# Batch 0's second half of x: one GpSimd transfer of four heads, or two of two heads

## The chip, the cores and the metric

The kernel runs on one core of a Trainium2 chip. The metric is device time in microseconds of one execution. The kernel before took 219.81 us in the median of three runs (219.65 to 220.38).

## What is computed

The reference has two stages. The first is attention in both directions between tokens x (8 batches, 8 heads, 512 tokens, 64 wide) and a small state (32 rows for each batch and head). The second is a feed-forward layer with a ReLU gate over all 8 x 544 rows of 512.

```
scores  = scale * x @ state^T      a  = softmax(scores)     xread = a  @ state
scores2 = scale * state @ x^T      a2 = softmax(scores2)    sread = a2 @ x
h   = concat(xread, sread) as 4352 rows of 512
out = (relu(h @ w_gate) * (h @ w_val)) @ w_out              # w_gate, w_val: 512 x 1536
```

## The kernel before, in words

The order of all work is written out by hand: a string of steps (L455 on) for the first part, then a loop with units at fixed places. Each engine executes its instructions in that order. The kernel never forms xread: it multiplies the state with the gate and value weights (`u_mm`, L291, into `U`) and applies the attention weights `ANS` to that (`gv_mm`, L323), gates the result (`relu` L351 on ScalarE, `mult` L356 on VectorE) and multiplies by `w_out` (L363).

The change lies in the prologue, which brings the first data in:

- Batch 0's x comes in two ways. Heads 0 to 3 are loaded as float32 in two transfers, from SyncE's and ScalarE's queues (L420), and cast to bfloat16 by ScalarE and VectorE (`x_conv_pair`, L144). Heads 4 to 7 are loaded by one transfer of GpSimd's queue, which casts on the way (L427).
- GpSimd then makes the identity matrix `id128` (L428, rows of masks.py) that all transposes on TensorE use, and issues the rest of the loads in this order: batch 1's x in two transfers of four heads (`x_load`, L430 to 434: steps `dx.1.0.2 dx.1.1.2`), the gate and value weights in column pieces of 128 and 256 (`w_dma`, L108 to 110: steps `dw`), batch 2's x (`dx.2.0.1`), the rest of the state (`ds`), and `w_out` (`do`).
- The transfers of GpSimd's queue take eight semaphores in turn. A transfer waits, at its issue, until the eighth one before it has landed.
- TensorE first runs warm-up matmuls (`spin`, L438), which compute nothing that is used; they stand between steps as well. It transposes the state (L123), then x in groups (`x_T`, L156 to 162): `xT.0.0.4` and `xT.0.4.4` for heads 0 to 3, score matmuls for these (`att_sc`, L172 to 179, `sc.0.0`), `xT.0.8.4` for heads 4 and 5, `xT.0.12.4` for heads 6 and 7, then `xT.1.0.8` for the first half of batch 1, `sc.0.1`, `sc.1.0`, `xT.1.8.8`, and the first products with weights (`c_unit`, L312: `c.0.0.128`, then `c.1.128.128`).
- VectorE and ScalarE copy each group out of PSUM (`x_out`, L165), take exponentials (L206), sums and reciprocals (L212, L214).

The four steps of the program's string that follow `sc.0.0` on TensorE are in these lines:

```
spin.1.384
xT.0.8.4@4 xT.0.12.4@5 xo.0.8.4.act xo.0.12.4.act spin.1 xT.1.0.8@6 sc.0.1@1 ex.0.1 xo.1.0.8.dve spin.1
```

Of the kernel before, what the change touches and what calls it, by code (L numbers as in the profile page):

```python
# [16 lines left out]
def kernel(  # L17
# [9 lines left out]
    nc = tc.nc  # L27

    B, H, S, D = x.shape
# [4 lines left out]
    NC = S // 128  # L34
# [21 lines left out]
    HK = H // NK  # L56
# [21 lines left out]
    xf, xb, xT, eT, e_sn, a_sn, ANS, U, hsb = {}, {}, {}, {}, {}, {}, {}, {}, {}  # L78
# [26 lines left out]
    def xb_alloc(b):  # L105
        xb[b] = att.tile([128, H, NC, D], BF16, name="xb", tag="xb", bufs=4)
# [317 lines left out]
        w_dma((moe_w_gate, moe_w_val)[w], (wg_sb, wv_sb)[w], lo, lo + n)  # L424

    xb_alloc(0)
    nc.gpsimd.dma_start(out=xb[0][:, HK:H], in_=x[0, HK:H].rearrange("h (p c) d -> p h c d", c=NC))  # L427
    make_identity(nc, id128)  # L428

    def x_load(b, part, parts):  # L430
# [172 lines left out]
```

## Time and profile before

| what | value |
|---|---|
| median of the runs | 219.81 us (219.65 to 220.38) |
| profiled execution, its own time | 219.39 us |
| its span, first to last instruction | 217.6 us |
| TensorE busy | 212.8 us, 98% of the span |
| VectorE, ScalarE, GpSimd busy | 135.0, 117.8, 42.5 us |
| granted TensorE clock | 1.000 |
| GpSimd's DMA queue | 9.05 MB, 31.0% of the 16 engines' span |

The profile shows one execution. A page lists busy time by engine, the span in 40 slices, the DMA queues, the chain of work that ended last, and groups of instructions; other views of the trace list instructions in order of time with what each waited for, or busy time in chosen stretches. PE is TensorE's matmuls, PEld its weight loads, DVE is VectorE, ACT ScalarE, POOL GpSimd, SP SyncE. "L162" is line 162 of the kernel. A row such as `2.67 1.50 POOL L434 ... x2` is a group that starts at 2.67 us and spans 1.50 us; brackets hold the idle time before it and what ended it. A DMA's issue is a short row on its engine; its landing is later, and is recorded by the semaphore that it raises.

### The profile page before, as it was taken

The page shows a single profiled execution, that of the slowest core. Times are in us where ns is not written, and L with a number is a line of the kernel's source. Part 1 is how long each engine was busy: PE and PEld are TensorE (multiplying, and loading weights), DVE is VectorE, ACT ScalarE, POOL GpSimd, SP SyncE. Part 2 cuts the span into 40 slices and gives each one's busy share as a digit, 9 for nine tenths or more (in the row PEclk, how much of TensorE's full clock was granted, in tenths as well). Part 3 has the DMA queues.
Part 4 walks back from the last instruction along what each step waited for, and adds up shares of the span by engine and source line. Part 5 has one row for each costly group of instructions (what it writes and reads, how often), then busy time and mean ns, then how long its engine had stood idle before and what let it go on. Part 6 is the DMA issues. An engine that isn't in the chain of part 4 may idle for free.

```text
span 217.6 us, 4865 instructions
## 1 busy us (share of the span) xinstructions
PE 212.8 (98%) x1952; PEld 104.8 (48%) x1952; DVE 135.0 (62%) x233; ACT 117.8 (54%) x225; POOL 42.5 (20%) x63
## 2 busy tenths in 40 slices
PE   8899999999999999999999999999999999999994
PEld 4554454454444444444444444444544445666543
DVE  4799967956887678557966796388745444222100
ACT  4798877747546556455555656454646443333221
POOL 7974049005600531020107000000000000000000
PEclk9999999999999999999999999999999999999999
DMA  7999999579963995919491453131311122222132
GB/s 168 180 196 197 202 221 171 78 139 188 152 175 74 144 186 110 167 52 193 99 148 60 110 134 96 49 99 50 84 28 51 48 48 50 61 56 80 51 96 96
DMA packets 47399, 24.96 MB, mean 115 GB/s; under 512 B 27824, under 2 KB 43056, under 8 KB 47376
## 3 DMA queue, kind: packets, MB, share of 16 engines
q0 software_dynamic: 16896, 9.05, 31.0%
q1 hardware_dynamic: 29584, 14.85, 28.7%
q10 hardware_dynamic: 896, 0.75, 1.3%
q8 instruction: 15, 0.25, 0.4%
q14 instruction: 8, 0.07, 0.2%
HBM read 18.35 MB, written 8.91 MB: 125 GB/s over the span
## 4 chain that ended last, share of the span: by engine, by line
PE 96%; DVE 1%; ACT 1%; issue 0%
PE o_ps L367 40%; PE gv_ps L325 38%; PE gv_ps L347 5%; PE up L298 4%; PE warm_ps L440 2%; PE upc L298 2%; PE o_ps L396 1%; PE sr_ps L265 1%; PE sc_ps L179 1%; PE sT_ps L189 1%; PE xT_ps L162 1%; ACT e_sn L206 1%; DVE xT L165 1%; ACT xT L165 0%; PE aT_ps L234 0%; DVE cs L212 0%
## 5 line engine op out<-in xcount | busy, mean ns | idle before, releaser
L367 PE MATMUL o_ps<-wo_sb,h_sb 128*128 128x512 bf16 x372 | 94.3, 379 | 0.0
L325 PE MATMUL gv_ps<-ans,U 128*128 128x512 bf16 x384 | 93.2, 379 | 0.0
L358 DVE TENSOR_TENSOR h_sb<-gv_ps,g_sb 128x512 bf16<-128x512 f32 x96 | 65.1, 688 | 42.8 <-ACT g_sb L354 41.3
L354 ACT ACTIVATE g_sb<-gv_ps 128x512 bf16<-128x512 f32 (+1 forms) x108 | 61.7, 578 | 51.4 <-PE gv_ps L325 39.1
L325 PEld LDWEIGHTS <-U 128*128 128x128 bf16 x384 | 37.1, 98 | 44.5 <-issue 0.8
L367 PEld LDWEIGHTS <-h_sb 128*128 128x128 bf16 x372 | 35.2, 98 | 42.0 <-issue 4.0
L310 DVE CAST U<-up 128x512 bf16<-128x512 f32 x44 | 27.7, 684 | 5.7 <-PE up L298 5.7
L375 ACT COPY o_sb<-o_ps 128x512 f32<-128x512 f32 x31 | 18.4, 594 | 19.7 <-PE o_ps L367 17.7
L310 ACT CAST U<-up 128x512 bf16<-128x512 f32 x28 | 14.7, 595 | 8.8 <-PE up L298 8.8
L254 POOL COPY xa<-xb 128x1024 bf16<-128x1024 bf16 x16 | 16.0, 1045 | 10.0 <-PE sr_ps L265 5.9
L358 DVE TENSOR_TENSOR hs_sb<-gv_ps,g_sb 128x256 bf16<-128x256 f32 x12 | 5.1, 425 | 15.3 <-PE gv_ps L347 10.4
L212 DVE TENSOR_REDUCE cs<-e_sn 128x16 f32<-128x512 bf16 x16 | 10.8, 677 | 1.1 <-ACT e_sn L206 1.1
L218 DVE TENSOR_TENSOR a_sn<-e_sn,rc 128x512 bf16<-128x512 bf16 x16 | 10.9, 687 | 0.4
L298 PEld LDWEIGHTS <-stT 64*32 64x32 bf16 x560 | 6.7, 91 | 6.4 <-issue 5.3
L320 ACT CAST U<-upc 128x512 bf16<-128x512 f32 (+1 forms) x19 | 8.7, 522 | 1.7 <-PE upc L298 1.7
L446 POOL COPY mark<-g_sb 128x1 bf16<-128x1 bf16 x4 | 0.8, 190 | 41.8 <-ACT g_sb L354 41.8
L197 ACT ACTIVATE eT<-sT_ps 128x512 bf16<-128x512 f32 x10 | 5.4, 594 | 5.3 <-PE sT_ps L189 5.3
L434 POOL DMA_DIRECT2D xb<-in_x_dram x8 | 6.8, 847 | 3.1 <-DMA wg_sb<-in_moe_w_gate_dram 1.4
L347 PE MATMUL gv_ps<-br,wg_sb 128*128 128x256 bf16 x48 | 7.2, 273 | 0.0
L347 PE MATMUL gv_ps<-br,wv_sb 128*128 128x256 bf16 x48 | 7.2, 273 | 0.0
L399 DVE COPY o_sb<-o_ps 128x64 f32<-128x64 f32 x2 | 0.4, 224 | 10.6 <-PE o_ps L396 10.5
L298 PE MATMUL up<-wg_sb,stT 64*32 64x512 bf16 (+1 forms) x168 | 6.9, 348 | 0.0
(59 smaller groups left out, 124.1 us busy)
## 6 DMA issues: line engine op xcount, KB each, us to landing
out_dram<-o_sb SPq DMA_DIRECT2D x26, 256.0 KB, 2.4
xb<-in_x_dram POOLq DMA_DIRECT2D x6, 512.0 KB, 7.1
wo_sb<-in_moe_w_out_dram POOLq DMA_DIRECT2D x2, 768.0 KB, 10.5
out_dram<-o_sb SPq DMA_DIRECT2D x11, 128.0 KB, 2.4
wg_sb<-in_moe_w_gate_dram POOLq DMA_DIRECT2D x5, 256.0 KB, 9.4
wv_sb<-in_moe_w_val_dram POOLq DMA_DIRECT2D x5, 256.0 KB, 10.0
xb<-in_x_dram POOLq DMA_DIRECT2D x3, 256.0 KB, 5.3
st_f<-in_state_dram POOLq DMA_DIRECT2D x1, 384.0 KB, 11.4
```

Of the source, the lines that this page charges most:

```text
L212: nc.vector.reduce_sum(out=cs, in_=e_v, axis=AX.X)
L218: {"dve": nc.vector, "pool": nc.gpsimd}[eng].tensor_tensor(out=a_sn[b][:, jp].rearrange("p c (j n) -> p c j n", n=Ns), in0=e_v, in1=held[" ...
L254: nc.gpsimd.tensor_copy(out=v[:, hs], in_=xb[b][:, hs])
L298: nc.tensor.matmul(dst[kc][i0:i0 + 32], stT[r:r + 64, parity, b, h], wsb[r:r + 64, j, lo:lo + n], start=True, stop=True)
L310: copy[eng](out=U[b][:, w, kc, lo:lo + 512], in_=held["u", b, w, lo][kc])
L320: copy[eng](out=U[b][:, :, kc, lo:lo + n], in_=held["c", b, lo][kc])
L325: nc.tensor.matmul(ps[w], U[b][:, w, kc, f0:f0 + 128], ANS[b][:, kc].rearrange("p c t -> p (c t)"), start=(kc == 0), stop=(kc == NK - 1))
L347: nc.tensor.matmul(ps[w][:, 0:nt], wsb[:, j, f0:f0 + 128], br[:, j].rearrange("p b n -> p (b n)"), start=(j == 0), stop=(j == NJ - 1))
L354: nc.scalar.activation(out=g_sb[:, 0:n], in_=ps[0][:, 0:n], func=AF.Relu)
L358: nc.vector.tensor_tensor(out=dst, in0=ps[1][:, 0:n], in1=held["g", b, jf][:, 0:n], op=ALU.mult)
L367: nc.tensor.matmul(held["o", b, tsub], src[:, jf, tsub * 128:(tsub + 1) * 128], wo_sb[:, jf], start=(jf == 0), stop=(jf == NF - 1))
L375: copy[eng](out=o_sb, in_=held["o", b, tsub])
```

## The change

One transfer of heads 4 to 7 becomes two: heads 4 and 5, then heads 6 and 7. Both are issued by GpSimd one behind the other, at the same place. The bytes and the tile stay the same, and all lines behind move down by one.

```diff
     xb_alloc(0)
-    nc.gpsimd.dma_start(out=xb[0][:, HK:H], in_=x[0, HK:H].rearrange("h (p c) d -> p h c d", c=NC))
+    for j in range(2, 4):
+        nc.gpsimd.dma_start(out=xb[0][:, 2 * j:2 * j + 2], in_=x[0, 2 * j:2 * j + 2].rearrange("h (p c) d -> p h c d", c=NC))
     make_identity(nc, id128)
```

## The prediction

> **What bounds the kernel now.** I read the page first: its engine table and its chain of work that ended last. TensorE is busy 98% of the span, and the chain lies on it for 96%.
>
> ```profile
> PE 212.8 (98%) x1952; PEld 104.8 (48%) x1952; DVE 135.0 (62%) x233; ACT 117.8 (54%) x225; POOL 42.5 (20%) x63
> ...
> PE 96%; DVE 1%; ACT 1%; issue 0%
> ```
>
> The time can change where TensorE still waits: the prologue. So I read the timeline of the first 30 us next (start, duration, engine, line, then what it waited for), and in it what GpSimd issues, and where TensorE meets x.
>
> ```profile
> 1.25 0.89 POOL L427 DMA_DIRECT2D xb<-in_x_dram x1 [0.81 <-POOLq L587]
> ...
> 2.13 0.22 POOL masks.py:197 MEMSET id<- 128x128 bf16 x1
> 2.43 0.29 POOL masks.py:199 TENSOR_SCALAR_AFFINE_SELECT id<-id 128x128 bf16<-128x128 bf16 x1
> ...
> 2.67 1.50 POOL L434 DMA_DIRECT2D xb<-in_x_dram x2
> ...
> 6.83 0.59 PEld L162 LDWEIGHTS <-xb 128*128 128x128 bf16 x8
> ...
> 7.96 0.45 PEld L162 LDWEIGHTS <-xb 128*128 128x128 bf16 x8 [0.48 <-DMA xb<-in_x_dram]
> ...
> 8.38 0.25 DVE L214 RECIPROCAL rc<-cs 128x16 f32<-128x16 f32 x1
> ...
> 8.66 0.69 DVE L165 COPY xT<-xT_ps 128x1024 bf16<-128x1024 bf16 x1
> ...
> 10.75 0.25 PE L298 MATMUL upc<-wv_sb,stT 64*32 64x128 bf16 x8
> ```
>
> L427 is the transfer that the change splits; the two of L434 are batch 1's halves. The weight loads at 6.83 are for batch 0's heads 4 to 7, and stand there with no wait. The next eight, for batch 1's heads 0 to 3, do wait for their DMA.
>
> Third, the stretches of 1 us (engines' busy time, clock, DMA share, GB/s):
>
> ```profile
> 3.00:4.00 1.00, 1.00 (x2) 0.10 (x1) 0.50 (x2) 0.17 (x1) 1.00 (x2) 1.00 1.10 373
> 4.00:5.00 1.00, 1.00 (x7) 0.61 (x6) 0.28 (x1) 0.63 (x2) 1.00 (x3) 1.00 1.39 202
> 5.00:6.00 1.00, 1.00 (x11) 0.90 (x9) 0.54 (x2) 0.57 (x1) 1.00 (x2) 1.00 1.42 190
> ```
>
> From 3 us on the DMA engines have more than one packet each in hand without a break (share over 1). So what lands when is set by the order and the bytes in GpSimd's queue, not by the moment of issue, as long as the queue holds work.
>
> Fourth, the trace's records of each transfer's semaphore give its landing: batch 0's heads 4 to 7 at 6.57; batch 1's halves at 7.92 and 9.25; the first four weight pieces of 128 KB at 9.98, 10.71, 11.46, 12.19; pieces of 256 KB at 13.53 and 14.86. Transfers of 256 KB follow each other by 1.33 to 1.35 us: the engines' rate, about 195 GB/s.
>
> **What TensorE can bear.** Heads 4 to 7 landed 0.26 us before TensorE came to them (6.83 - 6.57). Batch 1's first half has less room than its wait suggests. Its eight transposes end at about 8.59, and their copy on DVE starts at 8.66, behind a reciprocal that ends at 8.63; so some 0.05 us may be lost there before the path moves. The second weight piece landed at 10.71 and its matmul stands at 10.75, with some 0.08 us to spare before the score matmuls at 11.41, which wait for ACT. The fourth landed at 12.19, its matmul is at 12.26: 0.08 again. Hence a rule for this prologue: **if GpSimd's stream as a whole slips by d, the end moves by d less about 0.07 us; if it comes earlier, at most about 0.1 us is won**, since DVE and ACT are next.
>
> **The change, part by part.**
>
> Removed: one transfer of four heads (512 packets of 512 B, issue 0.89 us). Added: two of two heads, 256 packets each, the same bytes; one issue; 16 completion packets; one TensorE wait, ahead of the transposes of heads 6 and 7. Nothing is reordered: the instruction lists of the two kernels differ in that issue and wait, and in which semaphore each later GpSimd transfer uses.
>
> The added issue. Rows: 0.75 and 0.76 us for the next two transfers of 512 packets, 0.89 for the first, 0.75 for st_f's 384 packets. No row has 256. Bounds 0 and 0.89; I take 0.75, the nearest row. All that GpSimd does behind it moves 0.75 us later:
> - The identity is ready at 3.47 in place of 2.72. Its first reader is the state transpose, for which TensorE is free only at 4.53, when the warm-up matmuls end. Hidden, 1.06 us to spare; without the warm-up the cover would be the state's own load, which leaves 0.4.
> - Batch 1's first half is issued at 3.42, not 2.67. Its packets must be ready when the packets ahead run out. The packet records of GpSimd's queue show the first at 3.89, 2.64 us after the issue; four later transfers into an idle queue (issued at 51.7, 70.6, 84.4 and 107.4) needed 1.58 to 1.62. Fifteen of the sixteen engines pass on from the four heads at 5.25 to 5.60, the last at 6.24. At 1.60 the packets are there at 5.02, 0.23 us early: hidden. At 2.64 they are there at 6.06, and the fifteen run dry for 0.46 to 0.81 us. I take 1.60, because the 2.64 belongs to the first transfer of the program, which is still the same one.
> - Batch 1's second half (4.18) and the weight pieces (from 4.91) stand behind over 1 us of queued bytes each: hidden. GpSimd itself catches up where it waits for the eighth transfer before to land: 0.56 us before its issue at 13.81, 0.59 before 15.14.
> - The eight-deep reuse of semaphores keeps its distance: each later transfer waits for the same transfer as before. The two that newly wait for the halves, near 7.8 and 8.5, come after 6.57 either way, or wait hundredths.
>
> The added completion. Batch 0's transfer and batch 1's follow at 1.35, others at 1.33: 0.02 us for a boundary. The other end: two pieces of 128 KB take 0.72 to 0.75 each, together 0.13 more than one of 256 KB, though they also have twice the packets per byte, which the halves of x do not. Bounds 0 to 0.13, taken 0.02. Here a rule speaks against the change. The Trainium skill, "DMA: Bandwidth & Descriptors", section "Anatomy of one DMA — SWDGE (gpsimd) path", gives each such transfer a fixed 2.0 us beside its bytes, and "Rules for kernel authors" says to coalesce small transfers into a large one. Paid one after the other it would put 2 us on the sum by an estimate from that page; the trace disagrees, since transfers here land 0.72 us apart.
>
> The first packet may come a little earlier, as a smaller list is written: 0.89 less 0.75 is 0.14 us at most by the rows of issue. That is no gain, by the rule above.
>
> The added wait. The eight loads at 6.83 took 0.59 us with one wait among them, those at 7.96 and 9.63 0.45 and 0.46: bounds 0 to 0.13 us, taken 0, since the second half lands before the loads are reached. Behind it stand heads 6 and 7, a warm-up matmul, batch 1's transposes; the wait at 7.96 swallows up to 0.1.
>
> What the split gives: heads 4 and 5 land some 0.7 us sooner (128 KB at 195 GB/s), near 5.9. Nobody reads them before 6.83. Gain 0.
>
> Sum: d = 0.02, less 0.07 of room: 0. The profiled execution took 219.39 us (span 217.6), the median of the runs is 219.81. Sum on the first 219.4; on the median, which is what will be compared, **219.8**. All the bounds together, without a dry queue: -0.1 and +0.2 (0.13 + 0.13 - 0.07).
>
> **Rivals.**
> - A dry queue (slower). Place: GpSimd's queue at 5.25 to 6.1. It decides if batch 1's first transfer needs more than 1.83 us from issue to first packet (5.25 - 3.42). For: 2.64 at the program's start, where GpSimd issues without pause. Against: 1.6 in four later rows. Price 0.46 to 0.81, less 0.07: 220.2 to 220.55. About half of this lies beyond 0.3% (0.66 us).
> - A toll per transfer, paid in series. If a transfer's packets began only after the one ahead had landed, each boundary would cost the 1.1 us from data packets to landing (5.45 to 6.57) plus up to 1.6 to the first packet; for one boundary more, 220.8 to 222.4. The trace has packets of the next transfer running before the landing. This is the outcome of the page's rule named above.
> - A collision. If the shorter list starts the queue well before 3.89, it takes engine time from batch 0's heads 2 and 3, whose load lands at 4.70 and is cast on DVE at once; room to the weight loads at 5.39 is 0.2 us. At half the engines' time for 0.6 us, 0.3 us later: 219.9 to 220.1.
> - Faster. If in unprofiled runs the four heads land well after 6.83, TensorE stalls there now, and the split would put the first four transposes (about 0.3 us) and ScalarE's copy of them (two such take 1.07 us, so 0.54) under that stall: 0.3 to 0.84 us, 219.5 to 219.0. Against: 0.26 us of room in the one execution shown, and the larger gain needs a landing past 7.5.
> - That the first half lands no sooner can be too: one engine of sixteen ended 0.64 us behind the rest. It changes no time.
>
> **How the numbers follow.** What a measurement here can tell from no change is about 0.3%, 219.15 to 220.47. Forecast 0.60 (219.6 to 220.0); dry queue 0.22, half within and half beyond; toll 0.04, slower; collision 0.06, within; faster 0.08, beyond. So same 0.60 + 0.11 + 0.06 = 0.77, slower 0.15, faster 0.08. The range takes in the dry queue and the upper part of faster: 219.2 to 220.6. The runs shown alone spread from 219.65 to 220.38.
>
> **What would show it.** Right: two issues at L428 of 0.7 to 0.9 us, batch 1's issue near 3.4, landings still near 6.6, 7.9, 9.3 and 10.7, the weight loads at 6.83 and 7.96 where they are, and the span within a few tenths of 217.6. A dry queue would show as a landing of batch 1's first half past 8.3 and a longer DMA wait at 7.96, a toll as landings all shifted past 0.5 us, a collision as a later cast of x at L144. I am wrong if the path moves by more than the landings of GpSimd's queue do.

## The result, and the profile after

The changed kernel is slower: median 220.71 us (220.33 to 222.30, 8 runs) beside 219.96 us (219.65 to 220.50, 8 runs) for the kernel before, a ratio of 1.0045 with a 95% interval of 1.0025 to 1.0065. That is 0.75 us more where nothing was forecast, and 0.11 us past the top of the range. The ratio is an estimate over all runs and not the quotient of the two medians, which is 1.0034; microseconds below are differences of medians.

The profiled execution took 221.48 us, its span is 219.7 (before 217.6). The page's engine table and chain of work that ended last, with GpSimd's DMA in it for the first time:

```profile
PE 213.5 (97%) x1952; PEld 104.9 (48%) x1952; DVE 135.3 (62%) x233; ACT 118.1 (54%) x225; POOL 43.3 (20%) x64
...
PE 94%; DMA 3%; POOL 1%; DVE 1%; issue 1%; POOLq 0%
```

The timeline of the changed kernel (start, duration, engine, line, and in brackets the idle time before it and what ended it):

```profile
1.25 1.55 POOL L428 DMA_DIRECT2D xb<-in_x_dram  x2 [0.81 <-POOLq L588]
...
2.79 0.22 POOL masks.py:197 MEMSET id<- 128x128 bf16 x1
...
3.33 1.52 POOL L435 DMA_DIRECT2D xb<-in_x_dram  x2
...
6.50 0.60 PEld L162 LDWEIGHTS <-xb 128*128 128x128 bf16 x8
...
9.10 0.45 PEld L162 LDWEIGHTS <-xb 128*128 128x128 bf16 x8 [1.95 <-DMA xb<-in_x_dram]
...
9.77 0.69 DVE L165 COPY xT<-xT_ps 128x1024 bf16<-128x1024 bf16 x1 [1.46 <-PE xT_ps L162]
...
15.08 1.90 PE L325 MATMUL gv_ps<-ans,U 128*128 128x512 bf16 x8
```

The two issues take 1.55 us where one took 0.89, and GpSimd's stream, all that it issues behind, runs 0.66 us late from there. Batch 0's heads 4 to 7 are no trouble: their loads at 6.50 wait for nothing. The loads for batch 1's first half were at 7.96 after a wait of 0.48, and are now at 9.10 after one of 1.95. The last row, the first product with attention weights, stood at 13.01:

```profile
13.01 1.90 PE L325 MATMUL gv_ps<-ans,U 128*128 128x512 bf16 x8
```

That is 2.07 us, and the span grew by 2.09: all of the difference arises before this row. The stretches of 1 us show where (engines' busy time, granted clock, DMA share, GB/s); first the kernel before, then the changed one:

```profile
6.00:7.00 1.00, 0.67 (x12) 0.46 (x11) 0.48 (x2) 0.59 (x1) 1.00 (x2) 1.00 1.43 185
7.00:8.00 1.00, 0.85 (x11) 0.52 (x10) 0.34 (x1) 0.97 (x3) 1.00 (x3) 1.00 1.38 182
8.00:9.00 1.00, 1.00 (x17) 0.78 (x17) 0.93 (x3) 0.62 (x3) 1.00 (x2) 1.00 1.60 171
```

```profile
6.00:7.00 1.00, 0.86 (x15) 0.72 (x15) 0.08 (x1) 0.62 (x2) 1.00 (x2) 1.00 1.36 174
7.00:8.00 1.00, 0.49 (x6) 0.15 (x3) 0.67 (x1) 1.00 (x3) 1.00 (x3) 1.00 1.05 127
8.00:9.00 1.00, 0.00 (x0) 0.00 (x0) 0.27 (x2) 0.27 (x1) 1.00 (x2) 1.00 1.14 127
...
10.00:11.00 1.00, 0.66 (x12) 0.49 (x11) 1.00 (x3) 0.59 (x1) 0.42 (x2) 0.85 1.77 175
11.00:12.00 1.00, 1.00 (x9) 0.68 (x7) 0.93 (x4) 0.72 (x2) 1.00 (x2) 0.50 1.79 181
```

From 7 to 9 us the DMA engines move 127 GB/s instead of 171 to 182, while transfers that GpSimd has already issued wait behind. Not the whole of a transfer comes late. The trace records 16 semaphore updates for each transfer, and the landing is the last of them. Of the first half's 16, the eighth came at 7.19 (before: 7.12), the fourteenth at 7.24 (7.28), the fifteenth at 7.60 (7.50) and the last at 9.06 (7.92): TensorE waited for the slowest shares. TensorE stands still for all of 8 to 9 us, and then its granted clock falls: the clock records show half speed from 10.71 to 14.12 and full speed after. So the 2.07 us are 1.14 for the landing of batch 1's first half (7.92 before, 9.06 after, by the semaphores) and 0.93 that is left, which falls together with the halved clock. That the halved clock takes all of the 0.93 is not shown.

The halved clock is not in every run: of the 8 runs three (221.48, 222.26 and 222.30) have a mean granted clock of 0.990 to 0.992, the other five (220.33 to 220.76, median 220.38) 0.998 or more. Without it the change costs 220.38 - 219.96 = 0.42 us. The Trainium skill, "TensorE: Matmul & The Clock Gate", section "What's actually happening", says that the clock is set by windows of about 3.4 us of activity. The halved stretch here, 3.41 us long, agrees; that an idle window of about that length is needed first does not show here, since TensorE stood still for 1.62 us (7.49 to 9.11). In the change and in e4 (below), the two traces with a halved stretch, the clock records change at whole steps of 3.41 us: full at 3.88, half at 10.71, full at 14.12; in e4 4.31, 11.14, 14.55. In the step just ahead of the halving TensorE was busy for 1.46 of 3.41 us (7.30 to 10.71), in e4 for 1.11. In the other traces with clock records, no such step between the first full clock and 16 us has less than 2.17 busy (e1 and e10).

### The profile page after: what moved, and what is told of

Same layout as the page of the kernel before. It is cut to its first block, busy times and chain, and to the rows that moved or that the text cites. A ratio compares the mean times of both kernels' runs of the same rounds, so it can differ in the third digit from the quotient of the medians.

```text
span 219.7 us, 4866 instructions
## 1 busy us (share of the span) xinstructions
PE 213.5 (97%) x1952; PEld 104.9 (48%) x1952; DVE 135.3 (62%) x233; ACT 118.1 (54%) x225; POOL 43.3 (20%) x64
## 4 chain that ended last, share of the span: by engine, by line
PE 94%; DMA 3%; POOL 1%; DVE 1%; issue 1%; POOLq 0%
PE o_ps L367 40%; PE gv_ps L325 38%; PE gv_ps L347 5%; PE up L298 4%; DMA xb<-in_x_dram 3%; PE upc L298 2%; PE o_ps L396 1%; PE sr_ps L265 1%; PE xT_ps L162 1%; PE sT_ps L189 1%; PE sc_ps L179 1%; PE aT_ps L234 1%; POOL xb L428 1%; PE warm_ps L441 0%; DVE xT L165 0%
## 5 line engine op out<-in xcount | busy, mean ns | idle before, releaser
L325 PE MATMUL gv_ps<-ans,U 128*128 128x512 bf16 x384 | 93.2, 379 | 0.0
L325 PEld LDWEIGHTS <-U 128*128 128x128 bf16 x384 | 37.1, 98 | 44.5 <-issue 0.8
```

Source lines behind the costliest of these rows:

```text
L325: nc.tensor.matmul(ps[w], U[b][:, w, kc, f0:f0 + 128], ANS[b][:, kc].rearrange("p c t -> p (c t)"), start=(kc == 0), stop=(kc == NK - 1))
```

## The experiments

Two things came with the split: one transfer more, and 0.66 us of lateness for all that GpSimd issues behind. The theories are (a) the transfer itself costs, by its completion or its extra wait; (b) the lateness costs, because the queue's backlog does not cover it; (c) the queue is starved by something else, VectorE's use of memory or a fixed time from issue to first packet; (d) TensorE's halved clock costs. "First half" and "second half" below are batch 1's; "weights" the pieces behind them.

One table holds the edits' effect on the issues (us later than in the trace of before: 2.67, 3.43, 4.16), the landings of the first half and of the second weight piece (before: 7.92 and 10.71), the start of the first row of L325 (before: 13.01), each from one profiled execution, and the ratio to the kernel before over all runs, with its interval. The experiments stand in four groups (b1 with e5 to e7; e1 to e4; e9 to e12; e13 to e16), each on one chip with its own runs of the kernel before, whose medians were 219.73 to 219.91.

| run | first half, second half, weights issued later by | first half, weight piece landed | L325 | ratio |
|---|---|---|---|---|
| the change | 0.66, 0.67, 0.67 | 9.06, 11.86 | 15.08 | 1.0045 (1.0025 to 1.0065) |
| b1_before | 0.01, 0, 0.01 | 7.48, 10.28 | 13.12 | 0.9995 (0.9977 to 1.0012) |
| e1_split_again | 0.67, 0.68, 0.68 | 8.62, 11.68 | 13.71 | 1.0024 (1.0008 to 1.0040) |
| e2_split_id_later | 0.11, 0.68, 0.70 | 8.25, 11.35 | 13.38 | 1.0037 (1.0026 to 1.0048) |
| e3_one_delayed | 0.90, 0.91, 0.92 | 8.15, 11.60 | 13.64 | 1.0023 (1.0001 to 1.0046) |
| e4_four | 1.49, 1.49, 1.70 | 10.07, 12.81 | 15.89 | 1.0088 (1.0066 to 1.0109) |
| e5_one_id_later | -0.53, -0.02, 0.01 | 7.93, 10.79 | 12.98 | 1.0001 (0.9984 to 1.0017) |
| e6_weights_late | 0, 0, 0.60 | 7.51, 11.25 | 13.58 | 1.0002 (0.9989 to 1.0015) |
| e7_one_id_last | -0.54, -0.56, 0.14 | 7.97, 10.78 | 13.02 | 1.0002 (0.9975 to 1.0030) |
| e9_split_x1_early | 0.10, 0.11, 0.51 | 8.54, 11.40 | 13.59 | 1.0003 (0.9985 to 1.0021) |
| e10_x1b_late | 0, 0.55, 0.61 | 8.87, 11.65 | 13.92 | 1.0011 (0.9990 to 1.0032) |
| e11_dve_busy | 0, 0, 0 | 8.28, 11.08 | 13.32 | 0.9999 (0.9983 to 1.0014) |
| e12_x1b_later | 0, 1.49, 1.62 | 8.13, 11.93 | 13.96 | 1.0046 (1.0028 to 1.0063) |
| e13_bursts | -0.01, -0.01, -0.01 | 8.00, 11.25 | 13.28 | 1.0000 (0.9985 to 1.0015) |
| e14_weights_later | 0, -0.01, 1.50 | 7.62, 10.41 | 13.54 | 1.0044 (1.0023 to 1.0066) |
| e15_split_cover | 0.66, 0.67, 0.67 | 8.35, 11.71 | 13.75 | 1.0023 (1.0006 to 1.0040) |

One line joins the columns. L325 starts 5.05 us after the landing of the first half or 2.03 after that of the second weight piece, whichever is later, and not before about 13.0 to 13.1; and the span is that start plus 204.6. The two distances were fitted to these traces. The starts come out within 0.04 us in all but four of them: the change and e4 (halved clock), e6 (its state transposes began only at 4.82, where before has 4.32, and its clock was full only from 6.74), and e14, where the fourth weight piece (13.03) came last. The spans come out within 0.3, except e13's, whose edit is past that point. So landings ahead of 13 us decide, where TensorE itself is not late.

A single trace is not the median, though. b1_before is the kernel before again, and its weight piece landed 0.43 earlier than in the first trace; e13 has the same prologue as before, and there it landed 0.54 later (11.25). Both profiled runs of before, 219.39 and 219.53, are faster than the medians: a run takes 1.8 us more than its span, so by the line a run of 219.8 us would start L325 near 13.4 (an estimate: 219.8 - 1.8 - 204.6). e9 and e10 profiled later than their ratios say. Verdicts on times therefore rest on the ratios; what the traces say of the inside is one execution each.

Over all traces the stretch of 7 to 8 us goes with the issues: in the six with no issue more than 0.14 us late it has 166 to 196 GB/s, in ten of the twelve with one at least 0.5 us late 103 to 153. The other two are e10 (187) and e14 (193).

### The change again, and what lies in it

e1_split_again, the changed kernel measured a second time:

```diff
-    nc.gpsimd.dma_start(out=xb[0][:, HK:H], in_=x[0, HK:H].rearrange("h (p c) d -> p h c d", c=NC))
+    for j in range(2, 4):
+        nc.gpsimd.dma_start(out=xb[0][:, 2 * j:2 * j + 2], in_=x[0, 2 * j:2 * j + 2].rearrange("h (p c) d -> p h c d", c=NC))
```

> The changed kernel once more, for a second profile. If the late landing of batch 1's first half (9.06 us, against 7.92 before) belongs to the change, it lands past 8.3 here too, and the time is 0.3 to 0.9 us over the kernel before. If it was the chance of one execution (the DMA packets of 300 to 900 ns that stand in both traces), it lands near 7.9 and TensorE has no gap above 0.5 us there.

220.18 us beside 219.74: slower by 0.44, with no run below a clock of 0.998. The cost without the halved clock is thus found twice, 0.42 and 0.44, with an interval of 0.08 to 0.40% for the second. Here the fourteenth of the first half's 16 updates came at 7.46 and the last at 8.62.

e2_split_id_later: the split, with the first half issued ahead of the identity (against the kernel before, lines cut at "...").

```diff
-    nc.gpsimd.dma_start(out=xb[0][:, HK:H], ...
-    make_identity(nc, id128)
+    for j in range(2, 4):
+        nc.gpsimd.dma_start(out=xb[0][:, 2 * j:2 * j + 2], in_=x[0, 2 * j:2 * j + 2].rearrange("h (p c) d -> p h c d", c=NC))
...
+    x_load(1, 0, 2)
+    make_identity(nc, id128)
...
-    dx.1.0.2 dx.1.1.2 stc.0.1.dve ...
+    dx.1.1.2 stc.0.1.dve ...
```

> Two transfers, but batch 1's first half is issued ahead of the identity, so at about 2.8 us in place of 3.3 (2.67 in the kernel before); its second half and the weights stay as late as in the changed kernel. Issue theory (batch 1's first half is late because it is issued 0.66 us later): its landing comes back to about 8.0, and the time to within 0.2 us of the kernel before. Transfer theory (one transfer more costs the queue time in itself): landing and time stay as in the changed kernel, 0.4 to 0.9 us over before.

The first half is only 0.11 late, and the kernel is still slower by 0.37%. My first form of (b), that only the first half's lateness counts, fell here. The second half and the weights were 0.68 and 0.70 late.

e3_one_delayed: one transfer, with three fills of the identity's tile on GpSimd behind it, 0.66 us of work. All later issues come 0.90 us late by the table.

```diff
+    for _ in range(3):
+        nc.gpsimd.memset(id128, 0.0)
     make_identity(nc, id128)
```

> One transfer of four heads as before, and in the second one's place three GpSimd memsets of 128x128 (0.22 us each by the trace, with what lies between them 0.7 to 0.9), so that all issues behind are as late as in the changed kernel. Issue theory: as slow as the changed kernel, 0.4 to 0.9 us over before, batch 1's first half landing past 8.3. Transfer theory: as the kernel before, within 0.2 us.

Slower by 0.23%, with no second transfer. TensorE waits in another place, by the waits of e3 (engine, tile, line, releaser: us in total, times, longest):

```profile
PE upc L298 <- DMA wv_sb<-in_moe_w_val_dram: 0.5, 1, 0.5
```

It waits for a weight piece, where the changed kernel's trace waited for x: the first half landed at 8.15, not past 8.3 as expected. Lateness alone costs, though the interval (0.01 to 0.46%) only just leaves out nothing; e12 and e14 below are the clearer cases.

e4_four, four transfers of one head:

```diff
-    nc.gpsimd.dma_start(out=xb[0][:, HK:H], ...
+    for h in range(HK, H):
+        nc.gpsimd.dma_start(out=xb[0][:, h:h + 1], in_=x[0, h:h + 1].rearrange("h (p c) d -> p h c d", c=NC))
```

> Four transfers of one head in place of two of two: three issues more than before, batch 1's first half issued near 4.7 us. Issue theory: the queue runs dry for certain, it lands past 9, and the time is 1 to 2.5 us over before (more where TensorE's clock falls in the gap). Transfer theory with a toll T for each transfer: three tolls, about 3 times the loss of the changed kernel, also 1.2 to 2.5. Chance: as before.

Slower by 0.88%, 2.00 us beside 219.74; three of its six runs have a clock of 0.990 to 0.992. More lateness (1.49) costs more. The halved clock showed in three of these six runs, in three of the 19 of the change and e1, and in one of e12's twelve (222.17, clock 0.992); so few runs do not show that it comes more often. The timeline of e4:

```profile
10.11 0.45 PEld L162 LDWEIGHTS <-xb 128*128 128x128 bf16 x8 [2.63 <-DMA xb<-in_x_dram]
```

### Is it the transfer, or how late the issues come?

b1_before is the kernel before, unchanged, and gives the spread. e5_one_id_later and e7_one_id_last keep one transfer and issue the first half, or both halves, ahead of the identity.

> The kernel before once more, for a second trace of it: ratio 1 within 0.2%. If the slow stretch of GpSimd's queue (rate down to 80 to 150 GB/s between 7 and 9.5 us in all four traces with late issues, 163 to 190 in the one trace of before) belongs to the late issues, it is mild here too and the second weight piece lands near 10.7; if it is chance, it may be as deep here.

```diff
-    make_identity(nc, id128)
...
+    x_load(1, 0, 2)
+    make_identity(nc, id128)
...
-    dx.1.0.2 dx.1.1.2 stc.0.1.dve ...
+    dx.1.1.2 stc.0.1.dve ...
```

> The kernel before with batch 1's first half issued ahead of the identity (2.14 in place of 2.67 us); its second half and the weights are issued when they were. Issue theory in its first form (the lateness of batch 1's first half sets the time): a little faster, up to 0.3 us. In its second form (what counts is how late the second half and the weights are issued): no change within 0.2 us, the second weight piece landing near 10.7. Bandwidth alone: no change.

```diff
-    make_identity(nc, id128)
...
+    x_load(1, 0, 2)
+    x_load(1, 1, 2)
+    make_identity(nc, id128)
...
-    dx.1.0.2 dx.1.1.2 stc.0.1.dve ...
+    stc.0.1.dve ...
```

> The kernel before with both halves of batch 1 issued ahead of the identity (2.14 and 2.9 us); the weights as before. The identity is ready near 4.2, about when TensorE first needs it (4.3). Issue theory: the slow stretch gets milder and batch 1's second half lands up to 0.5 us sooner; time -0.3 to +0.1 us. Bandwidth alone: landings and time as before, or up to 0.3 us more if the identity comes late.

Half a microsecond earlier wins nothing: 1.0001 and 1.0002. The first half landed at 7.93 and 7.97, no sooner than in the two traces of before (7.92 and 7.48).

e9_split_x1_early keeps the split and takes the lateness away from both halves; VectorE zeroes the identity.

```diff
+    nc.vector.memset(id128, 0.0)
...
-    nc.gpsimd.dma_start(out=xb[0][:, HK:H], ...
-    make_identity(nc, id128)
+    for j in range(2, 4):
+        nc.gpsimd.dma_start(out=xb[0][:, 2 * j:2 * j + 2], in_=x[0, 2 * j:2 * j + 2].rearrange("h (p c) d -> p h c d", c=NC))
...
+    x_load(1, 0, 2)
+    x_load(1, 1, 2)
+    make_identity(nc, id128, nomemset=True)
...
-    dx.1.0.2 dx.1.1.2 stc.0.1.dve ...
+    stc.0.1.dve ...
```

> Two transfers as in the changed kernel, but both halves of batch 1 issued right behind them (about 2.8 and 3.55 us) and the identity afterwards, its zeroes written by VectorE, so that it is ready near 4.6. The weights stay 0.4 to 0.5 us later than in the kernel before, which alone cost nothing. Second-half theory (the loss is batch 1's second half being issued at 4.1 in place of 3.43): back to within 0.2 us of before, but for what the identity itself delays (up to 0.3 us, seen at the state transposes). Transfer theory (a third short transfer ahead of batch 1 disturbs the queue by itself): slow stretch and 0.4 to 0.9 us remain.

1.0003: the same split at no cost that can be measured. So theory (a) is not what costs most. It is not ruled out as a share: e9's interval reaches 0.21% and overlaps that of e1 (0.08 to 0.40%), and they ran on different chips. Its stretch of 7 to 8 us still shows a dip, a smaller one:

```profile
7.00:8.00 1.00, 1.00 (x18) 0.80 (x17) 0.00 (x0) 0.59 (x2) 1.00 (x2) 1.00 1.22 153
```

### Whose lateness

These keep one transfer, and let GpSimd fill padding columns with ones (the step `on`, moved up from later and repeated) at a chosen place. e6_weights_late has two fills ahead of the weights, e14_weights_later four; e10_x1b_late has two between the halves, e12_x1b_later four.

```diff
-    dx.1.0.2 dx.1.1.2 stc.0.1.dve ...
+    dx.1.0.2 dx.1.1.2 on on stc.0.1.dve ...
```

> The kernel before, with 0.4 to 0.8 us of GpSimd memsets (the step on, taken from later and made twice) between batch 1's second half and the first weight piece: x is issued as before, the weights as late as in the changed kernel. Issue theory, second form: the second weight piece lands about as much later as it is issued later (11.1 to 11.6 in place of 10.7), and the time rises by 0.3 to 0.7 us with batch 1's landings unchanged. Bandwidth alone (my prediction's ground): landings of the weights unchanged, since over 3 us of queued bytes lie ahead, and no change of time.

```diff
-    dx.1.0.2 dx.1.1.2 stc.0.1.dve ...
+    dx.1.0.2 on on dx.1.1.2 stc.0.1.dve ...
```

> One transfer of four heads, batch 1's first half issued as before (2.67), its second half 0.6 us later behind two GpSimd memsets (3.4 to 4.0), weights late too. Second-half theory: 0.4 to 0.6 us over before, second half landing past 9.8. Transfer theory: within 0.2 us of before.

```diff
-    dx.1.0.2 dx.1.1.2 stc.0.1.dve ...
+    dx.1.0.2 on on on on dx.1.1.2 stc.0.1.dve ...
```

> As the run with batch 1's second half late, with four memsets in place of two: its issue near 4.7. Second-half theory: twice the loss or more, 0.8 to 1.5 us over before, second half landing past 10.3. Transfer theory, or bandwidth alone: within 0.3 us of before.

```diff
-    dx.1.0.2 dx.1.1.2 stc.0.1.dve ...
+    dx.1.0.2 dx.1.1.2 on on on on stc.0.1.dve ...
```

> The kernel before with four memsets (1.3 to 1.6 us) between batch 1's second half and the first weight piece, x issued as before. Latency theory (a transfer here lands 5.9 us after its issue, as the second weight piece does in all 14 traces, 5.4 to 6.3): the second weight piece is issued near 6.4, lands near 12.2, and the time rises by 1.0 to 1.4 us. Bandwidth theory: the queue holds work until about 8.2, the weights' packets are ready near 7.4, so they land near 10.7 as before and the time stays within 0.2 us.

Weights 0.60 late cost nothing (1.0002), 1.50 late 0.44%. The second half with what follows costs 0.11% at 0.55, an interval that takes in both nothing and e3's cost, and 0.46% at 1.49. The expectations of a cost at 0.6 us thus missed in e6 and e10, and in e14 the expectations of both theories did: the second weight piece landed at 10.41, but the fourth only at 13.03, and the time rose. In e12 the first half was issued on time and the rate still falls, longer than in the changed kernel:

```profile
7.00:8.00 1.00, 0.95 (x15) 0.55 (x11) 0.20 (x1) 0.83 (x2) 1.00 (x3) 1.00 1.18 146
8.00:9.00 1.00, 0.82 (x17) 0.81 (x17) 0.89 (x3) 0.73 (x2) 1.00 (x3) 1.00 1.27 145
9.00:10.00 1.00, 0.70 (x12) 0.29 (x8) 1.00 (x2) 0.60 (x1) 1.00 (x2) 1.00 1.27 124
```

In e14, where both halves are on time and only the weights late, the rate from 7 to 8 us is undisturbed, and the dip comes at 11:

```profile
7.00:8.00 1.00, 1.00 (x20) 0.82 (x17) 0.10 (x1) 0.73 (x2) 1.00 (x3) 1.00 1.44 193
...
11.00:12.00 1.00, 0.63 (x11) 0.36 (x11) 0.96 (x3) 1.00 (x3) 1.00 (x2) 1.00 1.21 136
```

In these two traces the dip stands behind the late issue, but one trace each does not show that it always does: e10, with the same transfer late as e12, has its lowest rate from 6 to 7 us (151 GB/s), and e13, with nothing late in its prologue, has 162 from 5 to 6. What the times show is that no one transfer has the slack for 1.5 us: the second half with all behind it, or the weights alone, cost 0.44 to 0.46% without any split.

### What makes the queue thin

e11_dve_busy adds to the kernel before one product on VectorE (128x512, both inputs in on-chip memory, into a tile overwritten later) while GpSimd issues. In its trace it runs from 4.41 to 4.82 us, and so within the issue of the first weight piece (4.16 to 4.92).

```diff
+    def fill():
+        src = stT.rearrange("p r b h n -> p (r b h n)")
+        nc.vector.tensor_tensor(out=spare[:, 0:512], in0=src[:, 0:512], in1=src[:, 512:1024], op=ALU.mult)
...
-    dx.1.0.2 dx.1.1.2 stc.0.1.dve stc.0.0.dve dw.0.0.128 ...
+    dx.1.0.2 dx.1.1.2 stc.0.1.dve stc.0.0.dve fill dw.0.0.128 ...
```

> The kernel before with one extra VectorE operation of two operands in SBUF (128x512, about 0.7 us, its output overwritten later) from 3.9 to 4.6 us, while batch 1's second half is being issued. If late issues are costly because they fall into VectorE's busy time (4.8 to 6.1 us) and share a port of SBUF with it, the slow stretch shows here and the time rises by 0.3 to 0.6 us. Otherwise within 0.2 us of before.

0.9999. The Trainium skill, "SBUF — State Buffer", section "SBUF: two separate sides", warns that certain VectorE operations keep GpSimd from writing the lists for its transfers. This one cost nothing that can be measured, and the issue around it took its usual 0.76 us. It is another operation of VectorE that holds up an issue here, the cast of x from float32 (L144): in e11 it began 0.20 us into the next issue (4.89), which then took 0.93 us. So this run tests one product, and not VectorE's use of memory as such.

e13_bursts loads the later batches in four transfers each, into an idle queue, to measure the time from issue to landing.

```diff
-        x_load(b, 0, 1)
+        for part in range(4):
+            x_load(b, part, 4)
```

> A measurement, away from the prologue: the four late loads of x (batches 4 to 7, one transfer of eight heads each into an idle queue, 1.6 us to the first packet) are issued as four transfers of two heads, so with the shape of the split ones. If a transfer needs some 5.5 us from issue to landing whatever is queued (latency theory), the first of each burst of 128 KB lands 5 us or more after its issue. If latency is that of the idle queue plus bytes at rate (bandwidth theory), it lands after 1.6 + 0.7 + about 1 = 3.3 us, and the others 0.7 us apart. Time within 0.3 us of before: nobody waits for these loads at once.

The issues of e13 (line, engine, operation, count: min/median/max ns, first to last), and their landings:

```profile
L434 POOL DMA_DIRECT2D xb<-in_x_dram x16: 701/716/735, 52.6 to 110.6; - x16
...
DMA to landing us min/median/max: 2.9/3.7/5.1
```

An issue of two heads takes 0.72 us, which confirms that size. The first packet comes 1.40 to 1.56 us after an issue into the idle queue, and a first transfer lands 2.94 to 3.58 us after its issue. In e14 the first weight piece was issued at 5.66 and the second at 6.39, and the second landed at 10.41, 4.0 us after its issue; in the changed kernel the first half took 5.73. So there is no fixed time from issue to landing, and that form of (c) falls. The other form, VectorE, stays open by e11. In the changed trace no issue is held up (0.75 to 0.79 us for those of 3.33 to 7.03); whether a cast holds up something behind the issue was not tried.

e15_split_cover is the changed kernel with a longer warm-up filler on TensorE ahead of the loads for the first half; e16_split_third is the same once more, a single run.

```diff
-        xT.0.8.4@4 xT.0.12.4@5 xo.0.8.4.act xo.0.12.4.act spin.1 xT.1.0.8@6 ...
+        xT.0.8.4@4 xT.0.12.4@5 xo.0.8.4.act xo.0.12.4.act spin.4 xT.1.0.8@6 ...
```

> The changed kernel with four warm-up matmuls in place of one ahead of batch 1's first transposes, so that TensorE has no gap there long enough for its clock to be lowered. If the runs over 221.4 us are those in which the clock fell in the gap, there are none of these here, the clock reads 1.0 in the profile, and the median stays 0.4 to 0.7 us over before.

> The same kernel as the run with four warm-up matmuls, for a second trace of it: batch 1's first half lands between 8.2 and 9.1 and the second weight piece near 11.7, as in the two traces of the changed kernel.

220.18 us, as e1 without the filler, and 220.14 for e16's one run. No run of either had a clock below 0.998; but neither had e1, so whether the filler keeps the clock up is open. One of e15's runs took 221.63 at full clock: a time over 221.4 is not always the halved clock, as the expectation had it. The landings repeat, though: over e1, e15 and e16 the first half at 8.62, 8.35 and 8.71, the weight piece at 11.68, 11.71 and 11.51. By the rule above the weights end last in e1 and e15 and the first half in e16, by 0.04 to 0.34 us.

## Why the prediction was wrong

Its failed step is the term for the moved issues: "Batch 1's first half is issued at 3.42 ... hidden" and "Batch 1's second half (4.18) and the weight pieces (from 4.91) stand behind over 1 us of queued bytes each: hidden". It was taken as 0 and measured 0.42 and 0.44 us, 0.75 with the halved clock. In its place the runs showed that issues that come late can make the landings late while transfers issued long before still wait. Of the first half it is the last shares that come late: half of the first half's 16 updates came by 7.12 to 7.46 in all traces but those of e4 and e10. Point by point:

- **The issue**: 0.75 taken, 0.72 measured; the stream 0.66 later. Right. The identity was hidden too: the state transposes at 4.25 waited for VectorE's copy of the state.
- **The moved issues**: wrong. What lands when was said to follow from "the order and the bytes in GpSimd's queue, not by the moment of issue, as long as the queue holds work". It held work, and moved 127 GB/s in place of the 195 reckoned with. That lateness costs without a split is clear at 1.5 us (e12 and e14) and just clear at 0.9 (e3); e9 has the split, with x nearly on time, and no measured cost. That the 0.66 us of lateness is all of the change's cost is the likeliest reading, and not shown.
- **The completion and the added wait**: 0.02 and 0 taken. e9 bounds both together at -0.15 to +0.21%. Right as far as that reaches. The gain of 0 is right too: the split's halves landed at 5.38 and 6.04, and nobody reads them before 6.50.
- **The rule of slip**, "moves by d less about 0.07": right in form. Against the first trace of before the weight piece slipped by 0.80 to 1.00 in e1, e15 and e16, and L325 by 0.70 to 0.75. The room of 0.08 read for the second weight piece was too small: by the line it had 0.27 (13.01 - 10.71 - 2.03), and the first half 0.04.
- **The rivals**: the dry queue came nearest (220.2 to 220.55), with its place and condition wrong: not at 5.25 to 6.1, where the rate was 186 GB/s, but at 7 to 9, with the transfers issued from 4.10 on still waiting. Its share beyond 0.3% was also misread: 220.47 leaves about a quarter of 220.2 to 220.55 beyond it, not half. The toll in series fell with e9. The collision fell: the four transposes in question stand at 5.30 and no later than the 5.39 of before. The faster case fell with the result: the loads of the four heads wait for nothing, at 6.83 before as at 6.50 after.
- **What was missing**: that a wait this early can halve TensorE's clock. That rival was not there, and the runs that have it lift the median by 0.33 (220.71 - 220.38). The median of the other five, 220.38, lies inside the range only because the range takes in the dry queue, which is not what happened.

**Still open.** Why the rate falls while issued transfers wait: the traces show packets of 200 to 1300 ns where 60 is usual, and gaps, but not their source. Long packets are in every trace (one of 667 ns at 4.56 in before, none over 200 in b1_before), and there are more of them in most where issues are late. VectorE's float32 casts are a rival that no run here tests. And whether the split has a small share of its own: e2 (0.37%, split) and e10 (0.11%, not split) have nearly the same lateness, with intervals that overlap. No kernel run here beats the one before; e9 keeps the split at no cost that was measured.

## What to carry to other kernels

On a queue whose issuing engine is busy, count an added transfer as its issue time (0.72 us here) of lateness for everything issued behind it; here a backlog of over a microsecond did not cover 0.7 us of it, though 0.6 us of lateness for the weights alone was covered (e6). Only an experiment that delays without splitting, beside one that splits without delaying, tells the two apart. Find the first instruction after which all goes at a fixed distance (here L325, 204.6 us from the end), and read every edit by the landings ahead of it. Ask of a late landing whether the whole transfer or only its last share is late. Judge by medians, since single traces of one kernel differ by as much as the effect.

## What the runs showed of the hardware

- The issue of a transfer from GpSimd's queue depends little on its size: 0.54 to 0.69 us for one head (e4), 0.72 for two, 0.75 for four; the program's first took 0.69, 0.83 and 0.89.
- A stall of 1.62 us on TensorE was followed, 1.6 us after matmuls resumed, by 3.41 us at half clock; in e4 one of 2.30 us (2.63 at its weight loads, up to 10.11) by half clock from 11.14 to 14.55, again 3.41. Both halvings stand behind a step of 3.41 us in which TensorE was busy for 43% and 33%; steps with 64% and more (e1, e10) had none behind them.
- Where VectorE's cast of x (L144) began 0.03 to 0.22 us into a GpSimd issue, the issue ended 0.30 us after the cast's end, in all ten such traces, and took up to 0.95 us (e4). Where the cast began 0.24 to 0.33 us into one (e6, e9, e10), the cast took 0.68 to 0.73 us in place of 0.43, and the issue 0.74 to 0.76.
- The landing of a transfer is that of its slowest share: of 16 updates in the change 14 came by 7.24, the last at 9.06; in e4 eight by 7.74, the last at 10.07.
- With late issues and transfers waiting behind, the DMA engines fell to 127 GB/s for 2 us in the change and, in e4, to 81 from 8 to 9. The lowest of the split into two is e1's:

```profile
7.00:8.00 1.00, 0.90 (x13) 0.50 (x9) 0.26 (x1) 0.89 (x2) 1.00 (x3) 1.00 0.94 103
```
